# Linear attention and a highway layer on one core: wide warm-up products, sums and output tiles at other half steps, last rows stored in two parts

## The chip, the cores and the metric

The kernel runs on one NeuronCore of a Trainium2 chip. The metric is device microseconds from the start to the end of one execution; seven executions give a median of 149.52 us (149.28 to 152.77). A profile is taken from one execution, which has its own time (149.52 us) and a span, from its first to its last instruction (147.5 us). The core's engines are TensorE (PE, with PEld for its weight loads), VectorE (DVE), ScalarE (ACT), GpSimd (POOL) and SyncE (SP), which here only issues transfers.

## The reference

Two steps follow each other, for 8 batches, 8 heads, 576 positions and a head size of 64:

```python
q_s = softmax(q over d)            # per position
k_s = softmax(k over positions)    # per head and column
kv  = k_s^T v                      # 64 x 64 per head
att = q_s kv                       # 8 x 8 x 576 x 64
x   = att as 4608 rows of 512
H   = relu(x w_h)
T   = sigmoid(x w_t + b_t)
out = T*H + (1-T)*x                # 4608 x 512, float32
```

## The kernel before

**Attention, per batch.** q, k and v of a batch are loaded with heads split over two halves of the 128 partitions; 576 positions stand as 64 groups of 9. Exponentials run on ScalarE in two halves (`exp_half`, L150). VectorE sums q's exponentials per head in two halves (`q_sums`, L195), and the reciprocals scale q: for batches 0 to 2 on VectorE (`q_scale_v`, L202 to L208), from batch 3 on with a reciprocal on VectorE (`q_recip`, L211) and the product on GpSimd in two pieces (`q_scale_p`, L217). v is cast to 16 bits in two halves (`cast_v`, L157, on GpSimd), with a column of ones beside it, so that the product of k's exponentials with v (`kv_half`, 36 small products, tile psk) also yields k's sums; `kv_norm` (L182 and L184) divides by these. q is turned by TensorE in three groups (`q_trans`, tile pq) and copied out by VectorE (L231). `x_pair` and `x_left` multiply it by the normalized kv: eight position groups of a batch go into xT, transposed; three of four copies run on ScalarE (L253), the last on VectorE (L255). The ninth group of all batches is gathered in x9 (L268).

**Highway layer, per chunk.** A chunk is one batch's 512 positions, and a ninth chunk (index 8) is x9. For each of four column blocks: `gate` (4 products of 512 columns, tile pt, then tanh on ScalarE in place, L286), `carry` (4 products, tile ph, then VectorE's dd = max(ph,0) − x, L295) and `blend` (g = (tanh+1)·dd on VectorE, L303). `out_tile` turns x and g of a pair of batches back with identity products that add them up (eight products into the tile nat, of which there is one buffer), ScalarE copies the result (L329), and each fourth tile issues a store of 1 MB on SP. `turn9` does the same for x9 in four column blocks, into tiles that stay for all four; `finish9` copies them out (L348 on VectorE, L350 on ScalarE) and stores them.

**What sets the order.** The order on every engine is the program's own, written out by hand: work is put at numbered half steps with `at`, and the half steps are run through in turn. Chunk c and block ob have gate at 8c+2ob, carry at 8c+2ob+1 and blend at 8c+2ob+2. Batch b's attention stands in the half steps of chunk b−1: with p = 8(b−1), turning starts at p+2, kv at p+3, x at p+5 to p+7. The exponentials of its q start at p−4 (p−1 and p−2 for batches 1 and 2), those of its k at p. Within one half step, functions run in the order in which they were put: gates and carries, blends, output tiles, turn9, then batches in rising order, then loads. Each engine takes its instructions strictly in that order, so one that waits holds up all behind it.

**Ahead of the half steps** stands a list for batch 0: 70 products of 128 columns on the identity matrix (`warm_up`, written to a PSUM tile that nobody reads), batch 0's attention with 10 and 20 more of them between its steps, and the casts of both weight matrices (L111). The loads of batches 0 and 1 and of the weights are issued first, all on SP; each load of a later batch waits on SP for one of three buffers.

PSUM holds four buffers for pt and ph, three for pq, psk and px, and one for nat.

Of the kernel before, what the change touches and what calls it, by code (L numbers as in the profile page):

```python
# [9 lines left out]
FP32 = mybir.dt.float32  # L10
FP16 = mybir.dt.float16
# [7 lines left out]
def kernel(  # L19
# [10 lines left out]
    nc = tc.nc  # L30
    B, H, S, D = q.shape
    P = 128
    N9 = S // 64
    NM = N9 - 1
# [4 lines left out]
    def heads_view(t, b):  # L39
        return t[b].rearrange("(c x) (p n) d -> (x p) c (n d)", x=2, n=N9)  # L40

    pool = lambda name, bufs, **kw: ctx.enter_context(tc.tile_pool(name=name, bufs=bufs, **kw))
    consts = pool("consts", 1)
# [8 lines left out]
    og = pool("og", 2)  # L52
# [6 lines left out]
    mm = lambda o, l, r, st, sp: nc.tensor.matmul(  # L59
        o, l, r, start=st, stop=sp, skip_group_check=True  # L60
    )
# [7 lines left out]
    ident = consts.tile([P, P], FP16, name="ident")  # L69
# [14 lines left out]
    def load(b, which, queues=None):  # L84
        t = ld.tile([P, 4, N9, 64], FP32, tag=f"{which}32", name=f"{which}32_{b}")
        in32[which][b] = t
        view = heads_view(src32[which], b)
        queues = queues or [nc.sync]
        step = 4 // len(queues)
        for i, eng in enumerate(queues):  # L90
            c = i * step
            eng.dma_start(  # L92
                t[:, c : c + step].rearrange("p c n d -> p c (n d)"),
                view[:, c : c + step],
            )
# [3 lines left out]
    def load_weight(n, w, tag):  # L99
        t = ld.tile([P, 4, N9, 64], FP32, tag=tag, name=f"w32{n}")  # L100
        w32[n] = t.rearrange("p c n d -> p (c n d)")[:, 0:2048].rearrange(
            "p (k n) -> p k n", k=4
        )
        nc.sync.dma_start(w32[n], w.rearrange("(k p) n -> p k n", p=P))
# [10 lines left out]
    nc.sync.dma_start(brow, moe_b_t.rearrange("(k p) -> k p", p=P))  # L115
    load_weight("t", moe_w_t, "q32")
    load_weight("h", moe_w_h, "k32")
    for w in "qkv":
        load(1, w)


    make_identity(nc, ident)
# [12 lines left out]

    warm = ps_ht.tile([P, 512], FP32, tag="ht", name="warm")

    def warm_up(n):
        for _ in range(n):
            mm(warm[:, 0:P], ident, ident, True, True)  # L140


    ek, eq, psk, qsT = {}, {}, {}, {}
# [9 lines left out]
            AF.Exp,  # L153
        )

    def cast_v(b, a):
        nc.gpsimd.tensor_copy(  # L157
            v16s[b % 2][:, :, 2 * a : 2 * a + 2, 0:64],
            in32["v"][b][:, 2 * a : 2 * a + 2].rearrange("p c n d -> p n c d"),
        )  # L160
# [148 lines left out]
    rows = out.rearrange("(g p n) m -> g p n m", g=B // 2, n=N9)  # L309
# [6 lines left out]
    def flat(t):  # L316
        return t.rearrange("p k d -> p (k d)")
# [16 lines left out]
    nat9 = {}  # L334
# [6 lines left out]
            blk = lambda t: t[:, k_, 2 * g : 2 * g + 2].rearrange("p b d -> p (b d)")  # L341
            turn_block(nat9[g], k_, blk(x9), blk(g9))

    def finish9():
        for g in range(B // 2):
            o = og.tile([P, 512], FP32, tag="o9", bufs=4, name=f"o9_{g}")
            if g % 2:
                nc.vector.tensor_copy(o, flat(nat9[g]))  # L348
            else:
                nc.scalar.copy(o, flat(nat9[g]))  # L350
            (nc.sync, nc.scalar)[g % 2].dma_start(rows[g][:, NM, :], o)


    events = {}
# [1 line left out]
    def at(p, *fs):  # L356
        events.setdefault(p, []).extend(fs)

    E = lambda f, *a: (lambda: f(*a))

    for c in range(B + 1):
        for ob in range(4):
            p = 8 * c + 2 * ob
# [5 lines left out]

    for g in range(B // 2):  # L370
        p = 16 * (g + 1)
        step = 2 if g < B // 2 - 1 else 1
        for i in range(8):
            at(p + 1 + i * step - (step == 1) * (i == 7), E(out_tile, g, i))
    for k_ in range(4):
        at(8 * B + 2 * k_ + 2, E(turn9, k_))

    for b in range(1, B):
        p = 8 * (b - 1)
        s = p + {1: -1, 2: -2}.get(b, -4)  # L380
        if b > 1:
            at(s, E(exp_half, b, "q", 0))
        at(s + 1, E(exp_half, b, "q", 1), E(q_sums, b, 0))
        at(s + 2, E(q_sums, b, 1))
        if b <= 2:
            at(s + 2, E(q_scale_v, b))
        else:
            at(s + 2, E(q_recip, b), E(q_scale_p, b, 0))
            at(s + 3, E(q_scale_p, b, 1))
        s = p + {1: 2}.get(b, 0)  # L390
        at(s, E(exp_half, b, "k", 0), E(cast_v, b, 0))
        at(s + 1, E(exp_half, b, "k", 1), E(cast_v, b, 1))
        tr, kv, x = {1: ((3, 4, 5), (6, 7), (7, 7, 7))}.get(
            b, ((2, 3, 4), (3, 4), (5, 6, 7))
        )
        for i in range(3):
            at(p + tr[i], E(q_trans, b, i))
        at(p + kv[0], E(kv_half, b, 0))
        at(p + kv[1], E(kv_half, b, 1), E(kv_norm, b))
        at(p + x[0], E(x_pair, b, 0))  # L400
        at(p + x[1], E(x_pair, b, 1))
        at(p + x[2], E(x_left, b))
# [1 line left out]
        at(8 * max(b - 3, 0), *[E(load, b, w) for w in "qkv"])  # L404

    for f in [
        E(warm_up, 70),
        E(exp_half, 0, "q", 0), E(q_sums, 0, 0),
        E(exp_half, 0, "q", 1), E(q_sums, 0, 1),
        E(q_scale_v, 0),  # L410
        E(exp_half, 0, "k", 0), E(cast_v, 0, 0),
        E(exp_half, 0, "k", 1), E(cast_v, 0, 1),
        E(q_trans, 0, 0), E(q_trans, 0, 1), E(warm_up, 10), E(q_trans, 0, 2),
        E(warm_up, 20),
        E(kv_half, 0, 0), E(gate_bias), E(kv_half, 0, 1), E(kv_norm, 0),
        E(x_pair, 0, 0), E(x_pair, 0, 1), E(x_left, 0),
        *[E(cast_weight, "t", k_, nc.vector) for k_ in range(4)],
        *[E(cast_weight, "h", k_, (nc.gpsimd, nc.vector)[k_ // 3]) for k_ in range(4)],
        E(exp_half, 1, "q", 0),
    ]:  # L420
        f()
# [1 line left out]
        for f in events.pop(p, []):  # L423
            f()
    assert not events, events

    finish9()


# [28 lines left out]
```

## Time and profile before

| What | Value |
|---|---|
| median of 7 runs | 149.52 us |
| profiled execution, its own time | 149.52 us |
| its span | 147.5 us |
| TensorE busy | 121.9 us (83%) |
| VectorE busy | 105.8 us (72%) |
| ScalarE busy | 89.7 us (61%) |
| GpSimd busy | 42.3 us (29%) |
| mean granted TensorE clock | 0.941 |
| moved | 40.07 MB, 272 GB/s over the span |

Busy times of engines overlap. In the row of the clock each digit is one of 40 equal slices of the span (3.69 us), in tenths of full speed; the row of DMA is the mean busy share of its 16 engines. A line of the chain of waits gives start, length and what the chain ran through; it follows the last instruction back to what released it, and so on. A line of a stretch gives the busy time of each engine in it (with the number of instructions), the granted clock, DMA's share and its GB/s. A group that is named "L59" is a product of TensorE, since one helper issues nearly all of them; the tile's name tells which.

### The profile page before, as it was taken

What the parts mean: (1) busy time and instruction counts of PE and PEld (TensorE: products, weight loads), DVE (VectorE), ACT (ScalarE), POOL (GpSimd) and SP (SyncE); (2) the same over time, 40 slices, a digit from 0 to 9 for tenths busy, and PEclk for the clock granted to TensorE, in tenths of its full rate; (3) what the DMA queues carried; (4) which work ended last, traced back from release to release, by engine and by line L of the source; (5) the groups of instructions that cost most, each with busy time, mean ns of one, the idle gap of its engine ahead of it and who ended that gap; (6) DMA issues with size and microseconds to landing.
All of it is one profiled execution on the core that took longest, in us unless ns stands there. A gap on an engine that the chain in (4) does not pass through costs nothing.

```text
span 147.5 us, 3624 instructions
## 1 busy us (share of the span) xinstructions
PE 121.9 (83%) x1525; PEld 71.2 (48%) x1525; DVE 105.8 (72%) x195; ACT 89.7 (61%) x127; POOL 42.3 (29%) x37
## 2 busy tenths in 40 slices
PE   6957498777499878998898899979899999999500
PEld 6947122433164345455544654554555455577400
DVE  0494569995997996897699769959976756643600
ACT  3660439447806783998498579939972856556410
POOL 2006050702300088029406900960493000000000
PEclk9999856999969999999999999999999999999955
DMA  4999999999999999319998998700330070426195
GB/s 166 360 396 396 393 411 412 411 408 410 409 409 409 411 406 412 136 71 274 410 407 300 287 406 343 289 0 4 140 144 7 0 289 0 176 109 249 40 377 192
DMA packets 15527, 40.07 MB, mean 272 GB/s; under 512 B 660, under 2 KB 664, under 8 KB 14488
## 3 DMA queue, kind: packets, MB, share of 16 engines
q1 hardware_dynamic: 15224, 39.33, 69.5%
q10 hardware_dynamic: 288, 0.52, 1.0%
q8 instruction: 12, 0.20, 0.5%
q14 instruction: 3, 0.02, 0.0%
HBM read 30.41 MB, written 9.44 MB: 270 GB/s over the span
## 4 chain that ended last, share of the span: by engine, by line
PE 39%; DVE 24%; POOL 11%; issue 7%; DMA 6%; ACT 4%; POOLq 3%; SPq 2%; ACTq 0%
PE ph L59 13%; PE pt L59 12%; DVE r L195 10%; POOL eq L217 6%; DMA v<-in_v_dram 6%; PE nat L59 5%; POOL v L157 5%; PE psk L59 4%; DVE xT L255 3%; DVE dd L295 3%; POOLq L453 3%; DVE g L303 2%; PE pq L64 2%; PE px L59 2%; SPq L92 2%
## 5 line engine op out<-in xcount | busy, mean ns | idle before, releaser
L286 ACT ACTIVATE pt<-pt,bt 128x512 f32<-128x512 f32 x36 | 23.9, 663 | 23.6 <-PE pt L59 23.6
L59 PE MATMUL pt<-xT,w16t 128*128 128x512 f16 x128 | 36.1, 399 | 0.9 <-DVE w16t L111 0.7
L59 PE MATMUL ph<-xT,w16h 128*128 128x512 f16 x128 | 34.7, 396 | 0.0
L217 POOL TENSOR_TENSOR eq<-eq,r 128x1024 f16<-128x1024 f16 (+1 forms) x10 | 21.0, 2116 | 41.7 <-DVE r L211 41.7
L329 ACT COPY o<-nat 128x512 f32<-128x512 f32 x32 | 18.9, 590 | 12.4 <-PE nat L59 10.9
L303 DVE SCALAR_TENSOR_TENSOR g<-pt,dd 128x512 f16<-128x512 f32 x36 | 24.7, 685 | 1.6
L295 DVE SCALAR_TENSOR_TENSOR dd<-ph,xT 128x512 f16<-128x512 f32 x32 | 21.7, 678 | 5.6 <-PE ph L59 5.3
L195 DVE TENSOR_REDUCE r<-eq 128x18 f32<-128x1152 f16 x16 | 21.5, 1347 | 5.5 <-ACT eq L150 5.4
L157 POOL CAST v<-v 128x1152 f16<-128x1152 f32 x16 | 18.5, 1185 | 22.7 <-DMA v<-in_v_dram 22.7
L150 ACT ACTIVATE eq<-q 128x1152 f16<-128x1152 f32 x16 | 18.7, 1166 | 6.4 <-DMA q<-in_q_dram 6.4
L59 PE MATMUL nat<-half_i,g 128*128 128x128 f16 x144 | 19.9, 219 | 1.6 <-DVE g L303 1.6
L59 PEld LDWEIGHTS <-w16h 128*128 128x128 f16 x144 | 13.0, 100 | 14.2 <-issue 3.1
L150 ACT ACTIVATE ek<-k 128x1152 f16<-128x1152 f32 x16 | 18.4, 1160 | 1.5 <-DMA k<-in_k_dram 1.5
L59 PEld LDWEIGHTS <-w16t 128*128 128x128 f16 x144 | 12.2, 100 | 14.5 <-issue 4.0
L231 DVE COPY qsT<-pq 128x1024 f16<-128x1024 f16 (+1 forms) x24 | 13.2, 554 | 7.5 <-PE pq L64 7.5
L59 PE MATMUL nat<-ident,xT 128*128 128x128 f16 x128 | 17.7, 219 | 0.7 <-ACT o L329 0.7
L64 PE MATMUL pq<-ident,eq 128*128 128x128 f16 x144 | 12.5, 225 | 6.3 <-DVE eq L208 3.7
L253 ACT CAST xT<-px 128x512 f16<-128x512 f32 x24 | 13.5, 599 | 6.2 <-PE px L59 6.1
L59 PEld LDWEIGHTS <-g 128*128 128x128 f16 x144 | 14.1, 98 | 6.6 <-DVE g L303 2.1
L64 PEld LDWEIGHTS <-eq 128*128 128x128 f16 x144 | 9.6, 101 | 12.5 <-ACT ek L150 3.9
L59 PEld LDWEIGHTS <-xT 128*128 128x128 f16 x128 | 12.5, 98 | 3.7
L59 PE MATMUL psk<-v,ek 64*64 64x65 f16 x576 | 7.9, 197 | 2.6 <-POOL v L157 2.6
(37 smaller groups left out, 86.3 us busy)
## 6 DMA issues: line engine op xcount, KB each, us to landing
out_dram<-o SPq DMA_DIRECT2D x8, 1024.0 KB, 4.0
q<-in_q_dram SPq DMA_DIRECT2D x7, 1152.0 KB, 14.5
k<-in_k_dram SPq DMA_DIRECT2D x7, 1152.0 KB, 14.7
v<-in_v_dram SPq DMA_DIRECT2D x7, 1152.0 KB, 14.7
q<-in_q_dram SPq DMA_DIRECT2D x2, 576.0 KB, 4.0
k<-in_k_dram SPq DMA_DIRECT2D x2, 576.0 KB, 6.9
v<-in_v_dram SPq DMA_DIRECT2D x2, 576.0 KB, 8.7
w32t<-in_moe_w_t_dram SPq DMA_DIRECT2D x1, 1024.0 KB, 10.8
```

The lines of the kernel that those rows point to most:

```text
L59: mm = lambda o, l, r, st, sp: nc.tensor.matmul(o, l, r, start=st, stop=sp, skip_group_check=True)
L64: nc.tensor.matmul(o, i, ident, is_transpose=True, start=True, stop=True, skip_group_check=True,)
L150: nc.scalar.activation(dst[b][:, :, 2 * a : 2 * a + 2, :], in32[which][b][:, 2 * a : 2 * a + 2].rearrange("p c n d -> p n c d"), AF.Exp,)
L157: nc.gpsimd.tensor_copy(v16s[b % 2][:, :, 2 * a : 2 * a + 2, 0:64], in32["v"][b][:, 2 * a : 2 * a + 2].rearrange("p c n d -> p n c d"),)
L195: nc.vector.reduce_sum(qsum[b][:, :, h], eq[b][:, :, h, :], axis=AX.X)
L217: nc.gpsimd.tensor_mul(e, e, r.broadcast_to(list(e.shape)))
L231: nc.vector.tensor_copy(qsT[b][:, :, n0:n1, :], t[:, :, 0:w, :])
L253: nc.scalar.copy(dst, t[c])
L286: nc.scalar.activation(ps, ps, AF.Tanh, bias=bt2[:, ob : ob + 1], scale=0.5)
L295: nc.vector.scalar_tensor_tensor(dd, ps, 0.0, xv(ob), op0=ALU.max, op1=ALU.subtract)
L303: nc.vector.scalar_tensor_tensor(gv(ob), th, 1.0, dd, op0=ALU.add, op1=ALU.mult)
L329: nc.scalar.copy(o32[g, n // 4][:, n % 4, :], flat(t))
```

## The change

- Warm-up products become 512 columns wide: the moving operand is a new tile `wide`, set to zero by VectorE at the start. There are 20 ahead of batch 0 instead of 70 narrow ones, 2 and 6 where 10 and 20 stood, and 2, 4, 2, 2 and 2 more between `kv_half`, `x_pair`, `x_left` and the first gate.
- The load of batch 1's v is issued as two halves. Its k exponentials and the first half of its v cast move from p+2 to p+4; the second half of the cast goes to VectorE, at p+6.
- From batch 4 on the q exponentials, sums and scaling move one half step ahead (p−5 instead of p−4), and the k exponentials and v casts too (p−1 instead of p). For batch 3 these stay, but kv goes from p+3, p+4 to p+4, p+5, and x from p+5, p+6 to p+6, p+6.
- Output tiles of the first three pairs move one half step later, to even ones. Those of the last pair go two to a half step, at 65 to 68, where they stood one to a half step from 65 on, with two at 71.
- `finish9` runs in two parts: columns 0 to 383 at half step 71, ahead of the last blend and the last `turn9`, and columns 384 to 511 at 72. It issues eight stores instead of four.

```diff
-    for w in "qkv":
-        load(1, w)
+    load(1, "q")
+    load(1, "k")
+    load(1, "v", [nc.sync, nc.sync])
...
+    wide = consts.tile([P, 512], FP16, name="wide")
+    nc.vector.memset(wide, 0.0)
+
     def warm_up(n):
         for _ in range(n):
-            mm(warm[:, 0:P], ident, ident, True, True)
+            mm(warm, ident, wide, True, True)
...
-    def cast_v(b, a):
-        nc.gpsimd.tensor_copy(
+    def cast_v(b, a, eng=None):
+        (eng or nc.gpsimd).tensor_copy(
...
-    def finish9():
+    o9 = {}
+
+    def finish9(ks):
+        c = slice(128 * ks[0], 128 * ks[-1] + 128)
         for g in range(B // 2):
-            o = og.tile([P, 512], FP32, tag="o9", bufs=4, name=f"o9_{g}")
+            if g not in o9:
+                o9[g] = og.tile([P, 512], FP32, tag="o9", bufs=4, name=f"o9_{g}")
             if g % 2:
-                nc.vector.tensor_copy(o, flat(nat9[g]))
+                nc.vector.tensor_copy(o9[g][:, c], flat(nat9[g])[:, c])
             else:
-                nc.scalar.copy(o, flat(nat9[g]))
-            (nc.sync, nc.scalar)[g % 2].dma_start(rows[g][:, NM, :], o)
+                nc.scalar.copy(o9[g][:, c], flat(nat9[g])[:, c])
+            (nc.sync, nc.scalar)[g % 2].dma_start(rows[g][:, NM, c], o9[g][:, c])
...
-        step = 2 if g < B // 2 - 1 else 1
-        for i in range(8):
-            at(p + 1 + i * step - (step == 1) * (i == 7), E(out_tile, g, i))
+        if g < B // 2 - 1:
+            for i in range(8):
+                at(p + 2 + 2 * i, E(out_tile, g, i))
+        else:
+            for i in range(8):
+                at(p + 1 + i // 2, E(out_tile, g, i))
     for k_ in range(4):
         at(8 * B + 2 * k_ + 2, E(turn9, k_))
+    at(8 * B + 7, E(finish9, (0, 1, 2)))
+    at(8 * B + 8, E(finish9, (3,)))
...
-        s = p + {1: -1, 2: -2}.get(b, -4)
+        s = p + {1: -1, 2: -2, 3: -4}.get(b, -5)
...
-        s = p + {1: 2}.get(b, 0)
+        s = p + {1: 4, 2: 0, 3: 0}.get(b, -1)
         at(s, E(exp_half, b, "k", 0), E(cast_v, b, 0))
-        at(s + 1, E(exp_half, b, "k", 1), E(cast_v, b, 1))
-        tr, kv, x = {1: ((3, 4, 5), (6, 7), (7, 7, 7))}.get(
-            b, ((2, 3, 4), (3, 4), (5, 6, 7))
-        )
+        at(s + 1, E(exp_half, b, "k", 1))
+        if b == 1:
+            at(p + 6, E(cast_v, b, 1, nc.vector))
+        else:
+            at(s + 1, E(cast_v, b, 1))
+        tr, kv, x = {
+            1: ((3, 4, 5), (6, 7), (7, 7, 7)),
+            3: ((2, 3, 4), (4, 5), (6, 6, 7)),
+        }.get(b, ((2, 3, 4), (3, 4), (5, 6, 7)))
...
-        E(warm_up, 70),
+        E(warm_up, 20),
...
-        E(q_trans, 0, 0), E(q_trans, 0, 1), E(warm_up, 10), E(q_trans, 0, 2),
-        E(warm_up, 20),
-        E(kv_half, 0, 0), E(gate_bias), E(kv_half, 0, 1), E(kv_norm, 0),
-        E(x_pair, 0, 0), E(x_pair, 0, 1), E(x_left, 0),
+        E(q_trans, 0, 0), E(q_trans, 0, 1), E(warm_up, 2), E(q_trans, 0, 2),
+        E(warm_up, 6),
+        E(kv_half, 0, 0), E(gate_bias), E(warm_up, 2), E(kv_half, 0, 1), E(kv_norm, 0),
+        E(warm_up, 4),
+        E(x_pair, 0, 0), E(warm_up, 2), E(x_pair, 0, 1), E(warm_up, 2), E(x_left, 0),
+        E(warm_up, 2),
...
-
-    finish9()
```

## The prediction

> **What bounds the kernel now.** I read the page first, then the chain of waits, then the timeline around one batch, then tables of stretches for the two ends.
>
> ```profile
> PE 121.9 (83%) x1525; PEld 71.2 (48%) x1525; DVE 105.8 (72%) x195; ACT 89.7 (61%) x127; POOL 42.3 (29%) x37
> ...
> PEclk9999856999969999999999999999999999999955
> DMA  4999999999999999319998998700330070426195
> ```
>
> No engine is full over the span, so the limit differs by stage. DMA is saturated up to slice 16 (60 us), and the TensorE clock dips in slices 5 to 7 and 12. The chain shows what sets the middle. From psk (kv_half) of one batch to psk of the next, 13.35 us later, it reads:
>
> ```profile
> 97.39 0.48 PE psk L59 x36
> 97.87 0.97 PE pt L59 x4
> 98.84 0.11 PE pq L64 x2
> 98.95 0.41 PE psk L59 x36
> 99.36 0.98 PE ph L59 x4
> 100.37 0.69 DVE dd L295
> 101.06 1.26 DVE r L195
> 102.32 0.60 DVE g L303
> 102.92 0.60 DVE xT L255
> 103.52 1.32 DVE r L195
> 104.86 0.39 DVE r L211
> ...
> 109.60 1.10 POOL v L157
> 110.74 0.48 PE psk L59 x36
> ```
>
> It is a closed loop: TensorE, then VectorE's two sums and reciprocal, then GpSimd (scale 4.19 us, first cast 1.10), then TensorE waiting. The same piece stands at 57.37, 70.71 and 84.05. TensorE itself has about 12.15 us of work in such a period (13.35 less its waits of 0.20, 0.52 and 0.45 us), VectorE about 11.6.
>
> At the front, stretches cut where the clock changes:
>
> ```profile
> 14.20:17.61 3.41, 1.53 (x19) 0.60 (x16) 1.74 (x7) 1.66 (x3) 0.00 (x0) 1.00 1.03 382
> 17.61:21.02 3.41, 2.70 (x6) 0.74 (x7) 3.04 (x6) 0.07 (x1) 2.19 (x3) 0.50 1.04 411
> 21.02:24.43 3.41, 3.41 (x9) 1.21 (x8) 2.28 (x3) 3.13 (x4) 0.00 (x0) 0.50 1.04 411
> 24.43:27.85 3.42, 1.67 (x14) 0.86 (x13) 3.32 (x6) 2.38 (x3) 1.13 (x1) 1.00 1.04 412
> 38.08:41.50 3.42, 1.25 (x12) 0.66 (x11) 3.32 (x6) 2.06 (x3) 0.15 (x1) 1.00 1.04 407
> 41.50:44.90 3.40, 3.40 (x50) 1.95 (x48) 3.30 (x6) 0.00 (x0) 0.00 (x0) 0.50 1.04 411
> ```
>
> Read: stretch, length, PE, PEld, VectorE, ScalarE and GpSimd busy, granted clock, DMA share, GB/s. The clock changes only on a grid of 3.41 us. A stretch with TensorE busy 1.25 or 1.53 us is followed by one at half clock; after 1.67 it stayed full; back to full came only after a stretch busy throughout.
>
> At the end VectorE's last pair is dd 137.17 and g 137.97, the last copies start at 140.30, and 2 MB of stores drain from 140.3 to 145.7 at about 390 GB/s; the span ends 1.8 us later, at 147.5. The profiled execution took 149.52 us, 2.0 more than its span, and is the median of the 7 runs. I add the sum to it.
>
> **Front, warm-up.** The 90 narrow products before x_pair go; 20 wide ones stand at the start, 8 near q_trans, and 2+4+2+2+2 around kv_half and x. A 512-column product takes 0.43 us at half clock (ph 1.71 for 4) and 0.216 at full. The first waits for VectorE's new memset (not in the trace; half a 0.21 us row to twice it), so starts near 2.0. The narrow ones stayed slow until 7.37, so 12.5 wide ones are done by then and the rest by 9.0; transposes start at 9.81, waiting for VectorE: no cost. The 4 ahead of x_pair end about 15.05 where px began at 14.82: 0.2 us late, hidden because ScalarE waits for batch 1's q load until 20.95. Without that cover it costs 0.2. TensorE is then busy nearly all of 14.20 to 17.61, so the clock stays full and ph(0,1) ends at 22.9 instead of 24.8. That gains nothing: the next product, pq of batch 1, waits for VectorE's chain from the 20.95 load (sums 22.15 and 24.02, reciprocal 25.39, scale 26.04) until 26.88.
>
> Here a rule speaks against the row. The Trainium skill (TensorE: Matmul & The Clock Gate, "What's actually happening") says the clock halves after at least one idle window of about 3.4 us. The new gap, 22.9 to 26.9, holds no whole cell of the grid (24.43 to 27.85), so by the rule it stays full. By the rows it does not: 27.85 ends a cell with only 26.88 to 27.85 busy, 0.97 us, below both that fell. The measurement decides: half clock from 27.85 to 31.26, where before was full.
>
> **Front, batch 1.** The second v cast moves from GpSimd (in 26.7 to 29.6, hidden) to VectorE, between g(0,2) and dd(0,3). VectorE runs unbroken from 27.38 to 31.77 before. A 512-column cast takes 0.55 us (L111), so 1152 take 1.2. Queued behind it: dd(0,3), the psk half that reads it, rz, kvn, px. At full clock psk's second half starts at 33.0 instead of 31.94 and px at 34.2 instead of 33.20: +1.0. With half clock, pq1 takes 0.86, ph(0,2) 1.71, its dd starts 31.3, g(0,2) 32.1, cast 32.8, dd(0,3) 34.0, px 35.15: +1.95. The k exponentials behind tanh(0,2) run 29.4 to 31.6, before psk needs them. Splitting v's load adds one SP issue (0.4 us) while DMA limits that queue: nothing.
>
> Batch 2 takes part back. Its q chain is unchanged, and TensorE's pause (38.5 to 40.66) shifts 1.95 later, so 38.08 to 41.5 is busy until 40.4 and the clock stays full. Before, half clock there put ph(1,2)'s dd at 47.04; at full, VectorE's unbroken queue (dd, g, qsT, dd, qsT, g from 41.26 to 45.05, then qsT, rz, kvn) sets it at 45.85: −1.2. Front net: **+0.8**.
>
> **Middle.** Batch 3 delays kv_half and x_pair, and output tiles move to even steps. pq1 still waits for GpSimd until 56.28. Then pt, nat, pq, psk, ph, psk put psk's second half at 59.6, sums at 58.7 and 61.1, reciprocal at 62.5, GpSimd at 63.05 instead of 65.42. Both x pairs in one step cost TensorE 0.9 us (the second waits for ScalarE's copy of the first). psk of batch 4 comes at 69.55 instead of 70.71: **−1.16**.
>
> Batches 4 to 7 have sums one step earlier. From psk at 0: pt 0.41, nat 1.29, pq 1.80, psk 2.00, ph 2.41; VectorE kvn 2.74, sum 3.12, dd 4.38, sum 4.98, reciprocal 6.36, g 6.8, xT 7.4; GpSimd starts 6.9 and frees psk at 12.24. GpSimd leaves the loop. But xT now stands behind the second sum and reciprocal (before, xT went ahead of that sum): the next gate's fourth product waits until 8.13 where TensorE was there at 7.4. From 8.35: nat, ph, pt, nat, pq, ph, pq (4.5) to psk at 12.85. Period 12.85 instead of 13.345, three times: **−1.48**. Psk of batch 7 to the gate of left-over rows: 15.28 before, 15.4 after (**+0.1**). Output stores are one step later on SP, with loads of batches 6 and 7 behind them; these are not needed for over ten steps (q 6 issued near 66, exponential near 81): nothing.
>
> **Tail.** From the gate of left-over rows at 0 (126.02 before; the end is at 21.5). Batch pair 3's eight tiles go two to a step. There is one nat buffer, so the second waits for ScalarE's copy of the first: before, 137.14 nat, 137.62 copy, 138.26 nat gives 1.12 to 1.28 us from tile to tile, plus a tanh of 0.6 where one stands between. Steps start at 0, 1.3, 3.95, 7.15, 9.7 and 12.9 for ph(8,2). Then no tile is left to fill gaps: dd 13.96, g 14.75, turn9 waits until 15.5, ph(8,3) 15.95, dd 17.0, two 384-column copies of 0.5 on VectorE ahead of g, g 18.65, last turn9 19.4. The 128-column copies follow; ScalarE issues two stores between its own, the last at about 21. Only 256 KB are left to drain: data until 22.3, plus 1.8: 24.1. TensorE ends 7 us later, the drain shrinks by 4.4: **+2.6**. (Pairs at 1.12 throughout and no tanh between: +1.8; at 1.28: +3.3.)
>
> Sum: 0.8 − 1.16 − 1.48 + 0.1 + 2.6 = **+0.9**; 149.5 + 0.9 = **150.4 us**.
>
> **Rivals.** (a) Faster: the period falls to TensorE's own 12.15 because the gate does not wait for xT. Three times 0.7 less: 148.3. It decides below 12.55, where the sum is zero. For it: TensorE is the fullest engine; against: VectorE's order is written out, and xT stands behind 3.5 us of work that starts with kvn. (b) Clock as the rule says, full from 27.85: batch 1 costs 1.0 instead of 1.95: 149.4, no change. (c) The loop stays at 13.35 through another wait: 150.4 + 1.5 = 151.9. (d) The tail costs only 1.0, since stores start early: 148.8; against it, one nat buffer.
>
> **How the numbers follow.** Own case 0.41 (149.8 to 151.0), (a) 0.16, (b) 0.17, (c) 0.18, (d) 0.08. Runs of this kernel lie within about 0.3%, so no change is 149.07 to 149.97. Faster 0.24 = (a) + (d); same 0.18 = (b) and the edge of the own case; slower 0.58. The range runs from (a) to (c) with the tail's upper bound: 148.3 to 152.3.
>
> **What would show it.** Half clock in a stretch near 28 to 31 and none near 18; px of batch 1 one to two us later; psk to psk 12.85 without a GpSimd wait; alternating nat and copy in steps 65 to 68; little drain after the last store. Wrong if the clock's grid lies elsewhere, or if a period is under 12.5.

## The result

The changed kernel takes 150.44 us (median of 27 runs, 149.27 to 152.25), the kernel before 150.08 us (median of 64, 149.18 to 152.85); the ratio is 1.0031, with a 95% interval of 1.0009 to 1.0053. So it is slower by about 0.5 us. The ratio leaves out disturbed executions. The profiled execution took 150.93 us, with a span of 149.1 against 147.5 before: its difference of 1.6 us is larger than that of the medians, so lengths from these two traces need the runs below beside them.

The page of the changed kernel, the same rows:

```profile
PE 123.7 (83%) x1465; PEld 66.3 (44%) x1465; DVE 106.9 (72%) x199; ACT 89.5 (60%) x129; POOL 40.8 (27%) x36
...
PEclk9999999569879999999999999999999999999995
DMA  5999999999999999101999999920160060525545
```

The dip of the clock has moved from slices 5 to 7 to slices 8 and 9, and there is a second one in slices 11 and 12, where the kernel before had one in slice 12. The chain of waits in the middle, from one batch's psk to the next:

```profile
85.07 0.41 PE psk L59 x36
85.48 0.97 PE pt L59 x4
86.45 0.45 PE nat L59 x8
86.90 0.11 PE pq L64 x2
87.01 0.48 PE psk L59 x36
87.48 0.23 DVE rz L186 x2
87.71 0.45 DVE kvn L188 x2
88.17 1.26 DVE r L199
89.43 0.60 DVE dd L299
90.02 1.27 DVE r L199
...
91.32 0.38 DVE r L215
91.70 0.55 DVE g L307
92.24 0.61 DVE xT L259
...
92.89 0.38 PE pt L59
...
97.64 0.41 PE psk L59 x36
```

GpSimd is no longer in it, and psk to psk is 12.57 us (85.07 to 97.64) instead of 13.35 us. What is in it instead is VectorE's row from rz to xT, for which the last product of the next gate waits.

The front, in stretches cut where the clock changes in this execution; only the first is cut as in the trace of before, for comparison (columns: stretch, length, PE, PEld, VectorE, ScalarE, GpSimd, clock, DMA share, GB/s):

```profile
14.20:17.61 3.41, 3.41 (x60) 1.23 (x44) 1.37 (x5) 1.66 (x3) 0.00 (x0) 1.00 1.02 375
...
22.53:25.94 3.41, 0.79 (x4) 0.17 (x2) 3.09 (x3) 2.47 (x4) 0.00 (x0) 1.00 1.04 410
25.94:29.35 3.41, 1.31 (x10) 1.07 (x11) 3.31 (x7) 0.00 (x0) 1.15 (x1) 0.50 1.04 412
29.35:32.76 3.41, 3.41 (x16) 1.76 (x15) 2.36 (x4) 1.97 (x3) 0.00 (x0) 0.50 1.04 411
...
36.17:39.58 3.41, 1.86 (x18) 0.81 (x19) 1.81 (x9) 2.29 (x4) 2.17 (x2) 1.00 1.04 405
39.58:43.00 3.42, 3.42 (x9) 1.18 (x8) 3.39 (x4) 2.70 (x4) 0.00 (x0) 0.50 1.04 410
```

The wide products keep TensorE busy from 14.20 to 17.61, and the clock full through 18. Then TensorE is idle (0.79 us busy in 22.53 to 25.94), and half clock follows for two cells of the clock's grid of 3.41 us, 25.94 to 32.76. TensorE's next work, the turning of batch 1, starts at 28.04 and runs without a break to the end of these two. A third cell at half clock, 39.58 to 43.00, follows one with 1.86 us of work.

Three lengths make the two traces comparable, because the load of batch 1's q ends at another time in each execution (20.95 to 22.09 in those of this study). The *front* runs from batch 1's q exponential, which waits for that load, to the first sum of batch 3; the *middle* from there to the gate of the left-over rows; the *tail* from there to the end of the span.

| kernel | q exponential | to first px | front | middle | tail | span |
|---|---|---|---|---|---|---|
| before | 20.95 | 12.25 | 26.70 | 78.37 | 21.48 | 147.5 |
| after | 21.66 | 14.99 | 28.76 | 75.06 | 23.62 | 149.1 |

Front +2.1, middle −3.3, tail +2.1, load +0.7: together the 1.6 us of the spans. The lengths of the middle repeat to 0.03 us in every kernel below.

### The profile page after: what moved, and what is told of

It reads as the page before. It is cut to its first block, busy times and chain, and to the rows that moved or that the text cites. A ratio compares the mean times of both kernels' runs of the same rounds, so it can differ in the third digit from the quotient of the medians.

```text
span 149.1 us, 3513 instructions
## 1 busy us (share of the span) xinstructions
PE 123.7 (83%) x1465; PEld 66.3 (44%) x1465; DVE 106.9 (72%) x199; ACT 89.5 (60%) x129; POOL 40.8 (27%) x36
## 4 chain that ended last, share of the span: by engine, by line
PE 48%; DVE 26%; DMA 10%; ACT 5%; SPq 3%; issue 3%; POOL 2%; ACTq 0%; POOLq 0%; DVEq 0%
PE pt L59 15%; PE ph L59 14%; DMA q<-in_q_dram 10%; DVE r L199 10%; PE nat L59 9%; PE pq L64 5%; DVE dd L299 4%; PE psk L59 4%; DVE g L307 3%; DVE xT L259 2%; SPq L92 2%; ACT o L333 2%; POOL eq L221 2%; PE px L59 1%; DVE eq L212 1%
## 5 line engine op out<-in xcount | busy, mean ns | idle before, releaser
L307 DVE SCALAR_TENSOR_TENSOR g<-pt,dd 128x512 f16<-128x512 f32 x36 | 24.4, 679 | 1.5
L161 POOL CAST v<-v 128x1152 f16<-128x1152 f32 x15 | 16.8, 1146 | 23.7 <-DMA v<-in_v_dram 14.7
L59 PEld LDWEIGHTS <-w16t 128*128 128x128 f16 x144 | 12.8, 100 | 16.2 <-issue 3.2
L59 PE MATMUL warm<-wide,ident 128*128 128x512 f16 x40 | 11.7, 432 | 1.9 <-DVE wide L140 1.9
```

Source lines behind the costliest of these rows:

```text
L59: mm = lambda o, l, r, st, sp: nc.tensor.matmul(o, l, r, start=st, stop=sp, skip_group_check=True)
L161: (eng or nc.gpsimd).tensor_copy(v16s[b % 2][:, :, 2 * a : 2 * a + 2, 0:64], in32["v"][b][:, 2 * a : 2 * a + 2].rearrange("p c n d -> p n ...
L307: nc.vector.scalar_tensor_tensor(gv(ob), th, 1.0, dd, op0=ALU.add, op1=ALU.mult)
```

## Experiments: each part alone

The prediction's three parts were run one at a time, and a fourth kernel filled the gap in which the clock falls.

**The middle alone.** The kernel before, with the diff's lines for batches 3 to 7 and the even half steps:

```diff
-        s = p + {1: -1, 2: -2}.get(b, -4)
+        s = p + {1: -1, 2: -2, 3: -4}.get(b, -5)
...
-        s = p + {1: 2}.get(b, 0)
+        s = p + {1: 2, 2: 0, 3: 0}.get(b, -1)
...
+            3: ((2, 3, 4), (4, 5), (6, 6, 7)),
...
-        for i in range(8):
-            at(p + 1 + i * step - (step == 1) * (i == 7), E(out_tile, g, i))
+        if g < B // 2 - 1:
+            for i in range(8):
+                at(p + 2 + 2 * i, E(out_tile, g, i))
+        else:
+            for i in range(8):
+                at(p + 1 + i - (i == 7), E(out_tile, g, i))
```

> The kernel before with the middle part alone: sums, scaling, k exponentials and v casts of batches 4 to 7 one half step earlier, batch 3's kv and x later, output tiles of the first three pairs at even half steps. Theory (the two profiles: psk to psk 13.35 us before, 12.57 after, three times, and 1.0 us on the way to batch 4): 3.3 us faster than before, ratio 0.978, with psk to psk at 12.5 to 12.6 again. Rival (the gain in the profile came from being late: a stage that starts later finds its data ready): at most 1.5 us faster, ratio 0.99 or more, psk to psk at 13 or more.

Measured: 147.57 us against 150.31, ratio 0.9787 (0.9731 to 0.9844). Psk to psk is 12.57 us again (chain lines of psk at 69.50, 82.08, 94.64 and 107.21), the middle 75.06. The theory holds: 3.2 us, with its mechanism.

**The tail alone.**

```diff
-        for i in range(8):
-            at(p + 1 + i * step - (step == 1) * (i == 7), E(out_tile, g, i))
+        if g < B // 2 - 1:
+            for i in range(8):
+                at(p + 1 + 2 * i, E(out_tile, g, i))
+        else:
+            for i in range(8):
+                at(p + 1 + i // 2, E(out_tile, g, i))
...
+    at(8 * B + 7, E(finish9, (0, 1, 2)))
+    at(8 * B + 8, E(finish9, (3,)))
```

> The kernel before with the last pair's output tiles two to a half step and the last rows stored in two parts, nothing else. Theory (the waits for the one nat buffer in the profile of after, and a gate of left-over rows to end of 23.5 us against 21.5): 2.0 us slower, ratio 1.013. Rival (the earlier stores pay for it, and what after lost was lost at the front): no slower than before, ratio 1.000 or less.

Measured: 151.63 us against 150.31, ratio 1.0084 (1.0054 to 1.0114), 1.3 us slower; tail 23.14, that is 1.7 longer than before. The rival falls. The size is below the expected 2.0, because 0.5 of the 2.1 us by which the changed kernel's tail is longer belongs to the middle's edit: it moves the third pair's last tile past the gate at which the tail begins (the tail of the middle alone is 22.03 against 21.48).

**The front alone:** the wide products and the moves of batch 1.

```diff
-            mm(warm[:, 0:P], ident, ident, True, True)
+            mm(warm, ident, wide, True, True)
...
+    load(1, "v", [nc.sync, nc.sync])
...
-        s = p + {1: 2}.get(b, 0)
+        s = p + {1: 4, }.get(b, 0)
...
+            at(p + 6, E(cast_v, b, 1, nc.vector))
...
-        E(warm_up, 70),
+        E(warm_up, 20),
```

> The kernel before with the wide warm-up products, the halved load of batch 1's v and the moves of batch 1, nothing else. Theory: what is left of the sum, 0.45 + 3.3 - 2.0, about 1.7 us slower, ratio 1.012; between 1 and 2.8 by the profile (first sum of batch 3 at 50.4 instead of 47.65), with half clock somewhere in 26 to 33. Rival (the front's 2.8 us in the profile of after were one execution's late load and clock): ratio 1.000 to 1.003.

Measured: 152.12 us against 150.31, ratio 1.0124 (1.0073 to 1.0176). First px after 15.12 us, front 28.89 instead of 26.70; middle 78.39 and tail 21.52 are those of before. The changes of the three ratios, 0.9787, 1.0084 and 1.0124, add up to zero (−0.05%) where the changed kernel has +0.3%, within their intervals. The rival that the front's cost was one late load falls: it is there in another execution, and is counted from the load's end.

**The gap filled.** The changed kernel, with products on zeros ahead of batch 1's turning:

```diff
+    def fill(n):
+        t = ps_nat.tile([P, 512], FP32, tag="nat", name="fill")
+        for _ in range(n):
+            mm(t, ident, wide, True, True)
+
+    at(3, E(fill, 16))
```

> The changed kernel with 16 more wide products that nobody reads, between carry(0,1) and the first turning of batch 1, where TensorE stood idle for 4.7 us. Theory (the half clock of 26 to 33 us comes from that gap and costs about 1 us): full clock through 24 to 36, px of batch 1 about 1 us earlier against batch 1's q load than in after, and 0.7 to 1.2 us less than after, so a ratio to before of 0.996 to 0.999. Rival (VectorE's queue, with the cast in it, sets batch 1 whatever the clock): clock full, px no earlier, the time of after (1.003).

Measured: 149.50 us against 150.31, ratio 0.9953 (0.9926 to 0.9979): 1.2 us less than after by the two ratios. The trace, in stretches:

```profile
22.40:25.80 3.40, 3.40 (x18) 1.50 (x17) 3.00 (x3) 2.55 (x4) 0.00 (x0) 1.00 1.04 411
25.80:29.20 3.40, 2.68 (x19) 1.36 (x18) 3.30 (x7) 0.00 (x0) 1.15 (x1) 1.00 1.04 411
29.20:32.60 3.40, 3.40 (x59) 1.91 (x57) 3.40 (x7) 3.11 (x4) 0.00 (x0) 1.00 1.04 411
```

The clock is full up to 36.9 us, px comes 13.20 us after the q exponential instead of 14.99, and the front takes 27.04. Only products that nobody reads were added, 3.5 us of them, and the kernel became faster: the half clock of 26 to 33 us is what most of the front cost.

## Experiments: the front and the tail taken apart

**Wide products alone**, with batch 1 as in before:

```diff
-            mm(warm[:, 0:P], ident, ident, True, True)
+            mm(warm, ident, wide, True, True)
...
-        E(warm_up, 70),
+        E(warm_up, 20),
...
+        E(warm_up, 4),
+        E(x_pair, 0, 0), E(warm_up, 2), E(x_pair, 0, 1), E(warm_up, 2), E(x_left, 0),
+        E(warm_up, 2),
```

> The kernel before with the wide warm-up products alone. Theory (the front's 2.1 us, from batch 1's q exponential to the first sum of batch 3: 28.8 with the front's parts, 26.7 without, is mostly the clock, since filling the gap gave 1.7 back): full clock up to about 25 and half for 3 to 7 us after it, that stretch 1.2 to 1.7 us longer than in before, ratio 1.008 to 1.011. Rival (the cast in VectorE's queue makes most of it): half clock as well, but 0.5 us or less, ratio up to 1.003.

Measured: 151.63 us against 150.44, ratio 1.0058 (1.0020 to 1.0097). In its trace the clock is half from 27.2 to 30.6; first px comes after 13.51 instead of 12.25, and the front takes 27.35, 0.65 longer. That lies between the two expectations (1.2 or more against 0.5 or less): px is late by as much as the theory has it, but half of that is gone by batch 3's first sum.

**Batch 1's moves alone:**

```diff
-    for w in "qkv":
-        load(1, w)
+    load(1, "q")
+    load(1, "k")
+    load(1, "v", [nc.sync, nc.sync])
...
+        if b == 1:
+            at(p + 6, E(cast_v, b, 1, nc.vector))
```

> The kernel before with the moves of batch 1 alone (v load in halves, k exponentials two steps later, second half of the v cast on VectorE ahead of dd(0,3)). Theory: the clock falls at 18 and is back by 25 as in before, and the cast (0.81 us in the profile of after) lengthens VectorE's unbroken queue, so batch 1's q exponential to batch 3's first sum takes 27.2 to 27.5 instead of 26.7, ratio 1.003 to 1.006. Rival (the cast is most of the front): 28.2 or more, ratio 1.010.

Measured: 151.38 us against 150.44, ratio 1.0070 (1.0039 to 1.0100); first px after 13.25, front 27.16. The front is at the lower edge of the theory (27.2), the ratio just over its upper one. The rival's front of 28.2 did not come, though the interval of the ratio just reaches its 1.010. By their ratios, the wide products (0.58%) and these moves (0.70%) add up to the front alone (1.24%). The timeline of this kernel (start, length, engine, line, operation, result and operands; in brackets the idle time before and what ended it) shows two costs, not one:

```profile
25.52 1.15 POOL L158 CAST v<-v 128x1152 f16<-128x1152 f32 x1 [5.09 <-DMA v<-in_v_dram]
...
26.05 0.67 DVE L205 CAST r<-r 128x72 f16<-128x72 f32 x1
...
31.88 0.69 DVE L304 SCALAR_TENSOR_TENSOR g<-pt,dd 128x512 f16<-128x512 f32 x1
...
32.49 0.82 DVE L158 CAST v<-v 128x1152 f16<-128x1152 f32 x1
33.22 0.68 DVE L296 SCALAR_TENSOR_TENSOR dd<-ph,xT 128x512 f16<-128x512 f32 x1
33.36 0.48 PE L59 MATMUL psk<-v,ek 64*64 64x65 f16 x36 [0.63 <-DVE v L158]
```

The cast at 32.49 stands where the prediction put it, with dd and psk behind it. The other is the copy of the reciprocals at 26.05: 0.67 us instead of 0.20, as in the profile of the changed kernel (0.66). The first half of v lands sooner, so GpSimd's cast starts at 25.5 and runs while VectorE copies. A kernel with the same moves but v loaded whole tells whether that is it:

```diff
-    load(1, "v", [nc.sync, nc.sync])
+    load(1, "v")
```

> The moves of batch 1 alone, with v loaded whole as in before. Two costs showed in the moves: VectorE's cast of v (0.82 us), and VectorE's copy of the reciprocals, 0.67 us in every kernel with the halved load (GpSimd's cast then starts at 25.5, while it runs) and 0.20 in the others. Theory (the two engines get in each other's way): with v whole the copy takes 0.20, and batch 1's q exponential to the first px is 12.7 to 12.9 us, against 13.25 with the load halved and 12.25 in before. Rival (the copy's length comes from something else in the moves): 0.67 and 13.2 again.

Measured: the copy takes 0.20, first px comes after 12.76, and the time is 150.41 against 150.44, ratio 1.0024 (0.9986 to 1.0063).

```profile
26.57 0.20 DVE L205 CAST r<-r 128x72 f16<-128x72 f32 x1
...
27.54 1.70 POOL L158 CAST v<-v 128x1152 f16<-128x1152 f32 x1 [6.31 <-DMA v<-in_v_dram]
```

So halving the load made the copy longer, and of batch 1's 1.0 us to px, 0.5 is this and 0.5 the cast. In all four kernels with the halved load the copy ends 0.04 to 0.06 us after GpSimd's cast does (26.72 and 26.67 in the lines of the moves alone), and it is shortest, 0.59 us, where it begins latest in the cast (the front alone); so it seems to wait for the cast's end. With v loaded whole, GpSimd's cast is the longer one, 1.70 us instead of 1.15, beside VectorE's product that scales q. What the two engines contend for was not measured. The half us was not carried on to batch 3 in this execution, whose front takes 27.28 against 27.16, and the intervals of the two ratios overlap: what the halved load costs in time is not shown.

**The split of the last rows**, added to the middle alone, with the last pair's tiles one to a step:

```diff
-    finish9()
...
+    at(8 * B + 7, E(finish9, (0, 1, 2)))
+    at(8 * B + 8, E(finish9, (3,)))
```

> The middle part, and the last rows stored in two parts, with the last pair's tiles one to a half step as before. Theory (the doubled tiles make the tail longer, the split does nothing: ScalarE's copies of the first part still stand behind tiles 6 and 7, and 2 MB drain after them): the ratio of the middle alone, 0.977 to 0.981, and 21.3 to 22.2 us from the gate of left-over rows to the end. Rival (the split puts two copies ahead of VectorE's last product and is what costs): 23 us or more there, ratio 0.985 or more.

Measured: ratio 0.9794 (0.9733 to 0.9854), that of the middle alone; tail 21.69 against 22.03. The split costs nothing there, and the tail is 0.34 us shorter; the rival falls.

**The doubled tiles alone**, with the last rows stored whole; against the kernel of the tail alone:

```diff
-    at(8 * B + 7, E(finish9, (0, 1, 2)))
-    at(8 * B + 8, E(finish9, (3,)))
+    at(8 * B + 8, E(finish9, (0, 1, 2, 3)))
```

> The kernel before with the last pair's tiles two to a half step, and the last rows stored whole as in before. Theory (the doubled tiles wait for the one nat buffer and leave nothing to fill the last steps; storing in two parts is worth 0.3 us by the kernel with the middle and the split): the gate of left-over rows to the end takes 23.2 to 24 us instead of 21.5, ratio 1.009 to 1.016. Rival (the split's copies ahead of VectorE's last product are what made the tail longer): 21.5 to 22.5, ratio up to 1.006.

Measured: 153.14 us against 150.94, ratio 1.0190 (1.0089 to 1.0291); tail 24.39, 2.9 us longer than before and a little over what was expected. So with doubled tiles the split gives 1.25 back (24.39 to 23.14), more than the 0.34 where tiles still fill the last steps. The chain of waits of this kernel (start, length, what it ran through) shows TensorE and ScalarE taking turns:

```profile
127.80 0.46 PE nat L59 x8
...
128.33 0.59 ACT o L330
...
128.97 0.61 PE nat L59 x8
129.57 0.88 PE pt L59 x4
...
130.48 0.66 ACT pt L287
131.14 0.52 ACT o L330
...
131.70 1.05 PE nat L59 x16
```

A tile's copy must end before the next tile's products start, and every second copy stands behind a tanh that waits for a gate.

## Experiments: what bounds the middle now, and a faster kernel

**Another half step earlier.** In the middle alone:

```diff
-        s = p + {1: -1, 2: -2, 3: -4}.get(b, -5)
+        s = p + {1: -1, 2: -2, 3: -4}.get(b, -6)
```

> The middle part alone, with q's exponentials, sums and scaling of batches 4 to 7 one more half step earlier (p-6). Theory (the period of 12.57 us is set on VectorE: kvn, sum, dd, sum, reciprocal, g, and only then the xT that the next gate waits for): only one sum is left between kvn and xT, psk to psk falls to 12.1 to 12.4, and the kernel to 0.972 to 0.977 of before. Rival (TensorE's own work is the period now): psk to psk stays at 12.5 to 12.6 and the ratio at 0.979.

Measured: psk to psk falls to 12.30 us, as the theory has it (ph of the same step at 70.63, 82.93 and 95.24), but the ratio is 0.9801 (0.9738 to 0.9865), no better than 0.9787. The gain of 0.27 three times is lost on the way to batch 4, where, in the chain of waits, batch 4's two sums and its reciprocal now stand ahead of batch 3's kvn:

```profile
59.03 1.26 DVE r L196
60.29 0.59 DVE g L304
60.89 0.20 DVE qsT L232
61.09 1.27 DVE r L196
...
62.38 0.38 DVE r L212
62.76 0.55 DVE dd L296
63.30 0.14 DVE rz L183 x2
63.44 0.27 DVE kvn L185
```

Batch 3's last three px products start 15.98 us after its first sum (65.03), where they start after 15.18 in the middle alone: that is the 0.8 us of the three periods. The middle has the same length in both, 75.06 us. Theory and rival each got half.

**The parts that pay, together:** middle, wide products and the filled gap, batch 1 and tail as before. Added to the middle alone:

```diff
+            mm(warm, ident, wide, True, True)
...
+    at(3, E(fill, 16))
...
+        E(warm_up, 20),
```

> The middle part with the wide warm-up products and the 16 that fill the gap ahead of batch 1's turning; batch 1 and the tail as in before. Theory (the parts add up: middle -3.2, full clock through the front): batch 1's q exponential to batch 3's first sum in 25.5 to 26.5 us, mean clock 0.98 or more, and 0.3 to 1.0 us less than the middle alone, ratio 0.972 to 0.977. Rival (VectorE's queue alone sets the front): clock full, the time of the middle alone, 0.979.

Measured: 147.13 us against 150.44, ratio 0.9795 (0.9739 to 0.9851), not below the middle alone. First px after 12.24, front 26.02, full clock to 36.7, and a mean clock of 0.968 where 0.98 was expected. In before and in the middle alone, px comes as early (12.25 and 12.23): what half clock there was ahead of 24.4 us cost px nothing, and filling cannot gain what was not lost. So the rival is right on the time. But the narrow products do not always come off so well: the kernels of the middle with the split and with sums at p−6 have the same program up to there as the middle alone, and in their executions px came after 13.58 and 13.92. In these two the clock's grid lies elsewhere, and another cell of half clock (26.82 to 30.23, and 27.79 to 31.21) covers the turning of batch 1. In the three profiles with the gap filled, px came after 12.24, 12.24 (the next kernel) and, with batch 1's moves, 13.20.

**And the tail's real limit.** This adds the split, and stores the last pair's tiles by two:

```diff
+        if g == B // 2 - 1:
+            if n % 2:
+                j = n % 4 - 1
+                nc.sync.dma_start(
+                    rows[g][:, n - 1 : n + 1, :], o32[g, n // 4][:, j : j + 2, :]
+                )
+        elif n % 4 == 3:
```

> The middle part, wide warm-up products with 16 in the gap, batch 1 as before, last rows in two parts, and the last pair's tiles one to a half step but stored by two instead of four. Theory (after the last copies it is the 2 MB still to be stored that set the end): data of the last pair leave earlier, the gate of left-over rows to the end takes 20.3 to 21.3 us instead of 21.5, and the ratio is 0.970 to 0.976. Rival (the last copies and the receipt set the end): 21.5 or more, ratio 0.979.

Measured: 145.20 us against 150.44, ratio 0.9663 (0.9617 to 0.9710), a little better than expected, with a tail of 20.49. It beats both kernels: by about 5 us the one before, and by the ratios (0.9663 against 1.0031) the changed one by somewhat more. Two stretches, the first of before and the second of this kernel, both some 12 to 14 us behind the gate of the left-over rows, show what changed:

```profile
138.00:140.00 2.00, 1.05 (x16) 0.88 (x15) 1.54 (x3) 1.28 (x3) 0.00 (x0) 1.00 0.00 0
...
135.00:136.00 1.00, 0.48 (x8) 0.48 (x8) 1.00 (x4) 0.47 (x1) 0.00 (x0) 1.00 0.97 393
```

In before nothing is moved there, since the last 1 MB waits for its fourth tile; here half of it is already on its way. The end came 1.2 us sooner than with the split alone (21.69), so the drain of stores does set the end of before, and the rival falls: sending them in smaller pieces pays, crowding the tiles does not.

| kernel | to first px | front | middle | tail | ratio |
|---|---|---|---|---|---|
| middle alone | 12.23 | 26.05 | 75.06 | 22.03 | 0.9787 |
| tail alone | 12.24 | 26.69 | 78.38 | 23.14 | 1.0084 |
| front alone | 15.12 | 28.89 | 78.39 | 21.52 | 1.0124 |
| after, gap filled | 13.20 | 27.04 | 75.05 | 23.70 | 0.9953 |
| wide products alone | 13.51 | 27.35 | 78.38 | 21.48 | 1.0058 |
| batch 1's moves alone | 13.25 | 27.16 | 78.40 | 21.55 | 1.0070 |
| the same, v loaded whole | 12.76 | 27.28 | 78.37 | 21.43 | 1.0024 |
| middle and split | 13.58 | 27.42 | 75.06 | 21.69 | 0.9794 |
| middle, sums at p−6 | 13.92 | 27.69 | 75.06 | 22.09 | 0.9801 |
| middle, wide, gap filled | 12.24 | 26.02 | 75.05 | 22.02 | 0.9795 |
| the same, split, stores by two | 12.24 | 26.07 | 75.05 | 20.49 | 0.9663 |

(The doubled tiles alone have a tail of 24.39 and a ratio of 1.0190.)

The columns for px and the front come from one execution each. Six profiles have the narrow products and batch 1 as in before, and among these px comes after 12.23 to 13.92 and the front takes 26.0 to 27.7. So the fronts of the wide products alone (27.35) and of batch 1's moves alone (27.16) prove nothing by themselves; that these parts cost time rests on their ratios. The px of the changed kernel and of the front alone (14.99 and 15.12) lie outside that spread.

## Why the prediction was right, and where its terms were off

It forecast 0.9 us more, 0.6% slower, with three parts of which one gains; measured are 0.3%, or 0.5 us. The parts exist and have their signs, and each was shown alone; the mechanisms of the middle and the tail are those that were worked out, the front's only in part. Two things in the number are luck. The level: 150.4 against 150.44 fits so well because the kernel before has a median of 150.08 over 64 runs, not the 149.52 of the first seven (its runs spread from 149.18 to 152.85, far more than the 0.3% that the prediction allows). And the sum: in the two profiles the terms miss by +1.3 (front), −0.8 (middle) and −0.5 (tail), which cancel.

- **Middle, −2.54 foreseen, −3.3 measured.** The loop without GpSimd and the wait of the gate for xT behind two sums are in the chain in the order that was worked out. The miss is the period's: −2.33 in three periods instead of −1.48, since it is 12.57 us and not 12.85. The mis-sized piece is VectorE's row up to xT: the last product of the next gate starts 7.82 us after psk (85.07 to 92.89), where 8.13 was foreseen; from there to the next psk it takes 4.75, where 4.72 was foreseen. The way to batch 4 was close: −1.16 against −0.97 (psk at 72.51, less the 2.77 us by which this execution was late at batch 3's first sum).
- **Tail, +2.6 foreseen, +2.1 measured.** The steps came as worked out. VectorE's dd of the left-over rows stands at 8.3, 14.1 and 17.1 us after the gate at 125.48, where 13.96 and 17.0 were foreseen for the last two, and VectorE waits for them as it should:

```profile
139.60 0.69 DVE L299 SCALAR_TENSOR_TENSOR dd<-ph,x 128x512 f16<-128x512 f32 x1 [4.33 <-PE ph L59]
...
142.61 0.69 DVE L299 SCALAR_TENSOR_TENSOR dd<-ph,x 128x512 f16<-128x512 f32 x1 [1.52 <-PE ph L59]
```

  The last copies and the drain were 0.5 shorter than foreseen.
- **Front, +0.8 foreseen, +2.1 measured.** Two steps failed in size. The first is px of batch 1, 2.74 us late instead of 1.95. Half clock was put at 0.95 of this and cost 1.8 (14.99 to 13.20 where the gap is filled), with two slow cells instead of one: the clock's grid lay elsewhere, which the prediction named as a sign of being wrong. Batch 1's moves were put at 1.0 and cost 1.0 (13.25 against 12.25 with the moves alone), but only half of it is the cast, put at 1.2 us and measured at 0.81; the other half is the longer copy of the reciprocals, and the halved load behind it had been put at nothing. (The 512-column casts of 0.55 us, from which 1.2 was worked out, ran while GpSimd cast too.) The second step is "Batch 2 takes part back", put at −1.2 us: it is −0.7, with batch 3's first sum 2.06 late. A cell of half clock, 39.58 to 43.00, lies there as one did in before (41.50 to 44.90), and the prediction had full clock.
- **The clock, by the rows or by the rule.** For the new gap the prediction followed the rows and was right: the clock fell at 25.94, after a cell that was not idle (0.79 us of work) and 2.6 us after TensorE's last product. The rule would have given rival (b), 149.4, no change. But what the prediction read out of the rows is no rule either. A cell with 1.86 us of work (36.17 to 39.58) was followed by half clock, while one with 1.67 us kept it in before; in the first 55 us of all traces here, cells at full clock with 1.42 to 2.00 us of work kept it, and others with up to 2.07 us lost it. Nor does it take a cell that is busy throughout to come back: in the wide products alone 2.62 us at half clock (27.22 to 30.64) were enough, and in before 2.70 us were not.
- **Rivals.** (a), a period of TensorE's own 12.15, did not come: the wait for xT is there, though 12.57 is close to the 12.55 at which it would have decided. (c), the loop staying at 13.35, falls to the chain. (d), a tail that costs 1.0 since stores start early, is nearest in size for the tail alone in time (1.3), though the profile shows the waits that it denied.

Left open: what, besides the work in a cell, decides whether it loses the clock; why the grid lies differently from one execution to the next, while px of the same program, up to there, came up to 1.7 us later in one than in another; and how much of the spread of both kernels is due to it.

## What to carry to other kernels

A warm-up that keeps TensorE busy only until the next long wait can move the half clock behind that wait, where it meets work that counts; look at what each slow cell covers before removing it. In a kernel whose engines run a written order, moving a chain one step earlier can take the engine that waits for it (here GpSimd) out of the loop, but it puts the chain ahead of something else on its own engine (here xT), and that sets the next period. To empty a drain at the end, send smaller pieces sooner, rather than crowd the work that fills them through a single buffer.

## What was not expected of the hardware

Adding 16 products of 512 columns that nobody reads (3.5 us of TensorE) made a kernel 1.2 us faster. A 72-column copy on VectorE took 0.66 us instead of 0.20 when GpSimd's cast ran beside it, and ended just behind that cast. A cast of 1152 columns took 0.81 us on VectorE with GpSimd idle, where 512 took 0.55 beside GpSimd's casts. How busy TensorE was in a cell of 3.41 us did not decide alone whether the clock stayed full: it was lost after 1.86 us of work in the changed kernel and after 2.03 in the tail alone (14.86 to 18.27), and kept after 1.42 in batch 1's moves alone (22.24 to 25.66).
